# Projections behind the twelfth tile in quarters of the array, with row maxima in single banks beside them

## The chip, the cores and the metric

The kernel runs on one core of one Trainium2 chip. The metric is the device time of one execution, in microseconds. Times of the kernel before come from three runs; durations of single instructions come from one further execution, taken by the hardware profiler. The engines are called PE (TensorE, matrix products), DVE (VectorE), ACT (ScalarE), POOL (GpSimd) and SP (SyncE, which issues most transfers). PSUM has eight banks of 512 float32 for each of 128 partitions; "bank" below is one of these.

## What is computed

Two attention blocks over the same input x (2048 rows, 448 columns, 16 heads of 28), mixed row by row with a gate.

```python
g = sigmoid((x * gate_w).sum(-1))
# A: sliding local attention: 8 keys at distances 0, 2, .. 14
# B: full attention: every row against all 2048 keys
out = g * A(x, A_wqkv, A_wo) + (1 - g) * B(x, B_wqkv, B_wo)
```

Each block projects x with a 448 x 1344 matrix to queries, keys and values, takes a softmax of the scaled scores, and projects the result with a 448 x 448 matrix.

## The kernel before, in words

**Exactness.** PE multiplies in a short format, so every float32 operand is split into a high part (an ACT copy to that format) and a low part (the remainder, a subtraction on DVE or POOL). A projection is a sum of high x high, high x low and low x high.

**Stages.** After ten matmuls on zeros come the projections, then the main loop of 256 steps (scores at L1061, exponential on ACT at L1066, the product with V at L1027, with block A's work on DVE and POOL beside them), then the output projection (L895). An order written out by hand (`manual_schedule`) sets what each engine runs; each engine runs its instructions in the order in which the code writes them.

**Tiles.** The projections are 92 tiles, each 128 rows of PSUM by one bank. First 28 "qk" tiles (queries and keys of block B, transposed, 512 columns; 12 with weight set 0, 12 with set 1, 4 with set 2), then 16 "v" tiles (448 columns) and 48 "a" tiles (block A, 448 columns; the first 16 with two more for the gate). A tile is 11 products (`ORDER`) over the four pieces of the 448 input columns. The last tile is done by `last_tile` inside the main loop.

**Full and halves.** Tiles 0 to 9 (`FULL` = 10) use the whole array, a tile in one bank (`project`). From tile 10 on, `project_halves` splits each product in two of 64 rows, which run in the array's two halves side by side. The halves add into two banks of a pair `PJ`; there are 21 half products for a tile. ACT copies both banks out (L382 for qk, L403 for v and a), POOL adds the two halves (L384, L404, and L407 for the gate). For a qk tile ACT then makes the high part (L387) and POOL the low part (L388), one tile later, and two transfers store them.

**Row maxima.** Pass 1 of block B's softmax needs, for each of 1024 pieces (128 queries by 512 keys, one head), the maximum along the keys: one matmul (`s1_mm`, L153) into a bank and a DVE reduce. 320 of the 1024 are done beside the half products, four for each tile, as 64-row matmuls (`s1_half`): two on each half, in two-bank pairs `PM`, so one DVE reduce (L175) takes two banks. The other 704 run in the main loop (L153, reduces at L159). Every 64 maxima are combined (`max_parts`, L188 and L194 to L196) and turned and stored (`max_turn`, `max_store`).

**Weights.** Six further weight sets are loaded, and split by ACT (L240) and POOL (L241), tile by tile by the tables `loads` and `splits`.

## Time and profile before

| | |
|---|---|
| median of 3 runs | 895.21 us (895.15 to 895.33) |
| span of the profiled execution | 893.6 us |
| PE busy | 889.5 us, 100% |
| DVE busy | 742.3 us, 83% |
| ACT busy | 642.5 us, 72% |
| POOL busy | 642.6 us, 72% |
| first half tile on PE | about 31.4 us after the span's start |
| first main-loop matmul | 248.49 us |

The profiled execution's own time is its span; the times of the runs also hold what lies around it, 1.6 us here. A busy share is an average over stages with different limits, so the rows below are cut by stage. An instruction's duration in the trace runs from its start to its end; matmuls follow each other faster than that, since they are pipelined and run side by side in parts of the array. "Idle before" is an engine's idle time just before a group of instructions, with what ended it.

### The profile page before, as it was taken

The numbers are of one execution on the slowest core, as the hardware profiler recorded it, in microseconds if no ns is written. First come the engines' busy times: TensorE is split into PE (matmuls) and PEld (weight loads), VectorE is DVE, ScalarE is ACT, GpSimd is POOL, SyncE is SP. The second block draws the span as 40 slices with busy tenths as digits, with TensorE's granted clock in tenths as the row PEclk, the third lists the DMA queues.
The fourth block names the chain that finished last, engine by engine and source line by source line (L and its number), as shares of the span: only waits on it lengthen the run. The fifth ranks groups of instructions, "written<-read, shape, count | busy, mean of one in ns | idle before, by whom it ended". The sixth has DMA issues, their size and how long they took to land.

```text
span 893.6 us, 20540 instructions
## 1 busy us (share of the span) xinstructions
PE 889.5 (100%) x8318; PEld 530.0 (59%) x8318; DVE 742.3 (83%) x968; ACT 642.5 (72%) x765; POOL 642.6 (72%) x507
## 2 busy tenths in 40 slices
PE   9999999999999999999999999999999999999998
PEld 7889999999954444444444444444444444434997
DVE  7688999999979999999999999999999999832221
ACT  7456434343378898898988989989889898897220
POOL 1499856464469789998999989999999799701000
PEclk9999999999999999999999999999999999999999
DMA  8886403454372241225224322443121322437681
GB/s 262 267 284 180 157 12 84 135 138 124 100 252 66 90 137 48 65 64 154 74 56 141 89 58 90 126 95 102 46 61 32 92 43 46 107 79 212 179 279 52
DMA packets 114182, 104.51 MB, mean 117 GB/s; under 512 B 75256, under 2 KB 82424, under 8 KB 113304
## 3 DMA queue, kind: packets, MB, share of 16 engines
q1 hardware_dynamic: 113656, 102.42, 40.4%
q8 instruction: 65, 1.06, 0.5%
q10 hardware_dynamic: 432, 0.79, 0.3%
q14 instruction: 29, 0.24, 0.1%
HBM read 62.20 MB, written 40.96 MB: 115 GB/s over the span
## 4 chain that ended last, share of the span: by engine, by line
PE 99%; ACT 0%; issue 0%; DVE 0%; ACTq 0%
PE T L1061 31%; PE av L1027 28%; PE r L331 14%; PE r L326 8%; PE T L895 8%; PE r L153 5%; PE T L153 4%; PE r L226 1%; PE av L478 0%; ACT P L1066 0%; ACT onhi L952 0%; DVE res L1016 0%; ACT L L688 0%; ACTq L952 0%
## 5 line engine op out<-in xcount | busy, mean ns | idle before, releaser
L1066 ACT ACTIVATE P<-T 128x1024 f32<-128x1024 f32 x512 | 496.9, 1024 | 58.3 <-PE T L1061 56.1
L159 DVE TENSOR_REDUCE MX<-T 128x1 f32<-128x512 f32 x470 | 442.2, 953 | 31.3 <-PE T L153 18.8
L1027 PE MATMUL av<-P,V 128*32 128x512 f32 x2048 | 272.7, 605 | 0.0
L1061 PEld LDWEIGHTS T<-QH,KH 30*128 30x128 f32 x1024 | 92.2, 181 | 228.9 <-ACT P L1066 196.5
L153 PE MATMUL T<-KH,QP 30*128 30x512 f32 x704 | 220.9, 458 | 0.1
L1061 PE MATMUL T<-QH,KH 30*128 30x512 f32 x1024 | 211.3, 488 | 0.2 <-ACT P L1066 0.2
L175 DVE TENSOR_REDUCE MX<-r 128x2 f32<-128x1024 f32 x160 | 192.8, 1220 | 20.2 <-PE r L153 16.6
L1061 PE MATMUL T<-QH,KL 30*128 30x512 f32 x1024 | 185.7, 393 | 0.0
L1061 PE MATMUL T<-QL,KH 30*128 30x512 f32 x1024 | 183.0, 389 | 0.0
L662 POOL TENSOR_TENSOR prod<-qt,kt 128x896 f32<-128x896 f32 x64 | 135.4, 2115 | 4.4 <-DMA kt<-a_scr 4.4
L403 ACT ACTIVATE raw<-r 128x896 f32<-128x896 f32 (+1 forms) x62 | 57.1, 921 | 94.5 <-PE r L331 91.8
L153 PE MATMUL r<-KH,QP 64*128 64x512 f32 x320 | 112.9, 391 | 0.0
L723 POOL TENSOR_TENSOR oat<-oat,prod 128x896 f32<-128x896 f32 x48 | 101.4, 2112 | 2.0
L153 PEld LDWEIGHTS T<-KH,QP 30*128 30x128 f32 x704 | 86.0, 181 | 26.4 <-ACT P L1066 15.6
L331 PE MATMUL r<-wh,xh 64*128 64x448 f32 (+1 forms) x504 | 97.9, 363 | 0.0
L718 POOL TENSOR_TENSOR prod<-vt,L 128x896 f32<-128x896 f32 x56 | 95.5, 1706 | 0.3
L404 POOL TENSOR_TENSOR ast<-raw 128x448 f32<-128x448 f32 x47 | 54.3, 1155 | 56.3 <-ACT raw L403 45.8
L1061 PEld LDWEIGHTS T<-QL,KH 30*128 30x128 f32 x1024 | 93.9, 184 | 0.0
L1061 PEld LDWEIGHTS T<-QH,KL 30*128 30x128 f32 x1024 | 92.9, 182 | 0.2
L1027 PEld LDWEIGHTS av<-P,V 128*32 128x32 f32 x2048 | 40.3, 107 | 77.9 <-issue 65.3
L331 PEld LDWEIGHTS r<-wh,xh 64*128 64x128 f32 x504 | 77.5, 185 | 1.5
L331 PE MATMUL r<-wl,xh 64*128 64x448 f32 (+1 forms) x441 | 77.3, 365 | 0.0
(127 smaller groups left out, 1141.3 us busy)
## 6 DMA issues: line engine op xcount, KB each, us to landing
a_scr<-ast SPq DMA_DIRECT2D x24, 448.0 KB
qk_hi<-qkh SPq DMA_DIRECT2D x24, 256.0 KB
qk_lo<-qkh SPq DMA_DIRECT2D x24, 256.0 KB
rbc<-rs SPq DMA_DIRECT2D x64, 64.0 KB
QP<-qk_hi SPq DMA_DIRECT2D x64, 56.0 KB
KL<-qk_lo SPq DMA_DIRECT2D x16, 224.0 KB
QH<-qk_hi SPq DMA_DIRECT2D x64, 56.0 KB
QL<-qk_lo SPq DMA_DIRECT2D x64, 56.0 KB
```

The source lines that it names most:

```text
L153: nc.tensor.matmul(bank, qhis[u][h % 2][r, 128 * qs:128 * qs + 128], KH[u // NB % 3][r, 512 * kc:512 * kc + 512], start=True, stop=True)
L159: i = nc.vector.tensor_reduce(MX[:, n % NMX:n % NMX + k], bank, axis=X, op=ALU.max)
L175: nc.vector.tensor_reduce(m, PM[k], axis=X, op=ALU.max)
L326: nc.tensor.matmul(bank, ws[c][rows, k, t[4]:t[4] + 128], x, start=first, stop=last)
L331: nc.tensor.matmul(bank[:, 0:cols], x, ws[c][rows, k, 0:cols], start=first, stop=last)
L662: nc.gpsimd.tensor_tensor(out=p, in0=qt[c], in1=kvt["k", c % 2][:, HALO - DIL * w:HALO - DIL * w + NJ, :], op=ALU.mult)
L718: nc.gpsimd.tensor_tensor(out=dst.rearrange("p j (h d) -> p j h d", d=DH), in0=kvt["v", c % 2][:, HALO - DIL * w:HALO - DIL * w + NJ, :].r ...
L723: nc.gpsimd.tensor_tensor(out=ows[c % 2][:, :, 0:56] if w == W - 1 else oat[c], in0=oat[c], in1=oat[c, w], op=ALU.add)
L895: writes(bank, nc.tensor.matmul(bank[:, cols], src, wo[c][k][:, cols], start=(first and k == ks[0] and i == 0), stop=(last and k == ks[-1] ...
L1027: nc.tensor.matmul(av[32 * h:32 * h + 32, :], V[:, kt, 4 * g + h, :], tiles_[h], start=(kt == 0), stop=(kt == NJ - 1), skip_group_check=True)
L1061: nc.tensor.matmul(bank[a], (KH[g % 3], KH[g % 3], KL[g % 2])[t][r, ks], (qh, ql, qh)[t][r, :], start=(t == 0), stop=(t == 2))
L1066: e = nc.scalar.activation(p, one if a == "2" else mine, AF.Exp, scale=SCALE).ins
```

## The change

**Quarters.** `FULL` becomes 12. From tile 12 to 90 (79 tiles: 16 qk, 63 v and a) each product is split in quarters of 32 rows; 42 quarter products make a tile. All add into one bank. A tile visits the four quarters of the array one after the other, in an order that a planner (`quarters`) works out when the program is built, and up to six tiles are on their way at a time. Before the first product in the next quarter may write into the bank, the last one of the quarter that the tile leaves must be done: `product` puts a `nop` on POOL that waits for the one, and makes the other wait for that `nop` (`follows`), 237 times.

**Banks.** The PSUM tiles of the stage become eight single banks. A finished tile is copied by ACT straight to its place (`copy_tile`, L452; `qk_tile`, L446 and L447); nothing is added on POOL. The low parts of qk tiles and of weight sets 2 to 6 are made in two halves on POOL (`low_part`, L253), put into the order 32 and 42 products later, the stores 43 products later.

**Maxima.** The 320 maxima become 32-row matmuls, one quarter each (`s1_quarter`, L152), each into a bank of its own with its own reduce of 512 columns (L172).

**Loads.** The tables `loads` and `splits` move by some tiles; weight set 2 lives in the room of `KL[0]`. Two memsets are cut into pieces.

```diff
-        [128, 2, 512], F32, name=f"r{i}") for i in range(4)]
-    PJ, PM = PS[0:2], PS[2:4]
+        [128, 512], F32, name=f"r{i}") for i in range(8)]
...
+    def s1_quarter(h, bank):
+        n = 4 * count[h] + h
+        s1_mm(n, bank)
+        nc.vector.tensor_reduce(MX[:, n % NMX:n % NMX + 1], bank, axis=X, op=ALU.max)
+        count[h] += 1
...
+        def low_part(lo, raw, hi):
+            c = lo.shape[-1] // 2
+            for i, p in enumerate((slice(0, c), slice(c, lo.shape[-1]))):
+                soon(32 + 10 * i, lambda p=p: nc.gpsimd.tensor_tensor(
+                    out=lo[:, p], in0=raw[:, p], in1=hi[:, p].bitcast(F32), op=ALU.subtract))
...
+            rows = slice(0, 128) if q is None else slice(32 * q, 32 * q + 32)
...
+            if q is not None:
+                if n in moved:
+                    follows(i, moved.pop(n))
+                if leaves:
+                    moved[n] = nc.gpsimd.nop()
+                    follows(moved[n], i)
...
+        def quarter_order(n, q):
+            t = tiles[n]
+            low = (t[2] if t[1] == "qk" else t[-1] // 4) < 2
+            return [p for p in ORDER if p != (0, 1, 3) or q // 2 == (0 if low else 1)]
+
+        def quarters(n0, n1, maxima):
+            SLOT, LAT, COPY, FLIGHT = 552, 1030, 1400, 6
...
+                if b is not None and sent[q] < maxima // 4 and sent[q] == min(sent) and sums <= now_ + LAT + 900:
+                    sent[q] += 1
+                    sums = max(sums, now_ + LAT) + COPY + 40
+                    bank[b] = sums + 200
+                    cost = SLOT
+                    yield "max", q, b
...
+                        ready = [f for f in flying if f["in"] is None and f["left"][q] and f["next"] <= now_]
...
+                    if not f["left"][q]:
+                        f.update({"in": None, "next": now_ + (6 if tiles[f["n"]][1] == "qk" else 4) * SLOT})
...
-            raw = pair("raw")
-            nc.scalar.activation(raw, PJ[n % 2], AF.Copy)
-            r = raw[:, 0, :]
-            nc.gpsimd.tensor_tensor(out=r, in0=r, in1=raw[:, 1, :], op=ALU.add)
...
+            raw = ptile("raw")
+            nc.scalar.activation(raw, bank, AF.Copy)
+            nc.scalar.activation(hi, raw, AF.Copy)
+            low_part(lo, raw, hi)
+            soon(43, lambda: qk_store(nb, rows, hi, lo))
+
+        def copy_tile(bank, dst):
+            nc.scalar.activation(dst, bank[:, 0:D].rearrange("p (c e) -> p c e", e=dst.shape[-1]), AF.Copy)
...
-        FULL, S1_START = 10, 10
+        FULL, MAXIMA = 12, 320
...
-        loads = {2: 12, 3: 16, 4: 26, 5: 40, 6: 56}
-        splits = {1: (9, 2), 2: (20, 2), 3: (24, 2), 4: (34, 1), 5: (48, 1), 6: (64, 1)}
+        loads = {2: 10, 3: 13, 4: 22, 5: 38, 6: 54}
+        splits = {1: (9, 2), 2: (15, 2), 3: (18, 1), 4: (33, 1), 5: (48, 1), 6: (64, 1)}
```

**On PE, among the a tiles.** r0 and r1 are the pairs `PJ`, r2 and r3 the pairs `PM`; x2 to x7 are neighbours that alternate between the two halves. Before:

```order
L331 MATMUL r1_132<-wh5_1802,xl2_193 128x448
L153 MATMUL r3_140<-KH0_151,QP11_160 128x512 x2
L331 MATMUL r1_132<-wh5_1802,xl2_193 128x448 x5
L331 MATMUL r0_128<-wh5_1802,xh0_187 128x448 x4
L153 MATMUL r2_136<-KH0_151,QP10_159 128x512 x2
L331 MATMUL r0_128<-wh5_1802,xh0_187 128x448 x4
L331 MATMUL r0_128<-wl5_1803,xh0_187 128x448 x7
L331 MATMUL r0_128<-wh5_1802,xl0_191 128x448
```

And now; r0 to r7 are the eight single banks, and neighbours work in different quarters:

```order
L350 MATMUL r3_140<-wh4_1984,xl2_209 128x450
L350 MATMUL r6_152<-wh4_1984,xh1_204 128x450
L350 MATMUL r2_136<-wh4_1984,xl1_208 128x450
L350 MATMUL r0_128<-wh4_1984,xh3_206 128x450
L152 MATMUL r7_156<-KH0_167,QP00_173 128x512
L350 MATMUL r6_152<-wl4_1985,xh1_204 128x450
L350 MATMUL r1_132<-wh4_1984,xh3_206 128x450
L350 MATMUL r0_128<-wl4_1985,xh3_206 128x450
L350 MATMUL r3_140<-wh4_1984,xl2_209 128x450
L152 MATMUL r5_148<-KH0_167,QP00_173 128x512
```

A maximum stands alone among the products of four tiles, where two stood together between those of one or two.

**On DVE, in the middle of the stage.** Before, the reduces alternate between the two pairs:

```order
L175 TENSOR_REDUCE MX_154<-r2_136 128x2
L175 TENSOR_REDUCE MX_154<-r3_140 128x2
L175 TENSOR_REDUCE MX_154<-r2_136 128x2
L175 TENSOR_REDUCE MX_154<-r3_140 128x2
L175 TENSOR_REDUCE MX_154<-r2_136 128x2
```

And now, by single banks that the planner found free:

```order
L172 TENSOR_REDUCE MX_170<-r7_156 128x1
L172 TENSOR_REDUCE MX_170<-r0_128 128x1
L172 TENSOR_REDUCE MX_170<-r7_156 128x1
L172 TENSOR_REDUCE MX_170<-r0_128 128x1
L172 TENSOR_REDUCE MX_170<-r7_156 128x1
L172 TENSOR_REDUCE MX_170<-r4_144 128x1
L172 TENSOR_REDUCE MX_170<-r0_128 128x1
```

Mostly two banks alternate here; in the whole stage 228 of the 320 maxima go to the bank of the maximum two before.

**On ACT, at the first qk tiles of the new stage.** Before, one raw copy of two banks and one high part for each tile, with the splits of weight set 2 between:

```order
L240 ACTIVATE wh2_817<-raw_525 128x128 x2
L382 ACTIVATE raw_852<-r0_128 128x1024
L387 ACTIVATE qkh_809<-raw_810 128x512
L240 ACTIVATE wh2_817<-raw_525 128x128
L240 ACTIVATE wh2_817<-wt_526 128x128
L382 ACTIVATE raw_890<-r1_132 128x1024
```

And now, for six tiles that end within 60 matmuls of each other:

```order
L446 ACTIVATE raw_787<-r1_132 128x512
L447 ACTIVATE qkh_786<-raw_787 128x512
L446 ACTIVATE raw_787<-r4_144 128x512
L447 ACTIVATE qkh_814<-raw_787 128x512
L446 ACTIVATE raw_845<-r5_148 128x512
L447 ACTIVATE qkh_844<-raw_845 128x512
L321 ACTIVATE KL0_169<-raw_467 128x128 x2
L446 ACTIVATE raw_845<-r2_136 128x512
L447 ACTIVATE qkh_852<-raw_845 128x512
```

The raw copy is of one bank, the high part stands right behind it, and the splits (now into `KL0`) stand among six tiles in a row. From the first main-loop matmul on, every engine's rows are the same as before.

## Rows read from the trace of the kernel before

**Rows 1.** Windows by stage; busy us and count per engine, PEclk, DMA share, GB/s.

```profile
11.10:31.40 20.30, 20.30 (x89) 16.33 (x87) 13.76 (x21) 13.37 (x25) 1.04 (x2) 1.00 0.88 281
31.40:83.60 52.20, 52.20 (x451) 43.99 (x452) 43.25 (x38) 29.75 (x45) 46.02 (x41) 1.00 0.81 252
83.60:248.40 164.80, 164.80 (x1575) 160.84 (x1571) 151.28 (x135) 66.39 (x86) 98.41 (x105) 1.00 0.39 109
248.40:893.60 645.20, 641.84 (x6178) 301.45 (x6177) 526.36 (x757) 526.78 (x597) 492.92 (x354) 1.00 0.37 101
```

**Rows 2.** Groups of 31.4 to 248.4: count, busy us, mean ns, idle before.

```profile
L175 DVE TENSOR_REDUCE MX<-r 128x2 f32<-128x1024 f32 x160 | 192.8, 1220 | 20.2 <-PE r L153 16.6 <-PE r L326 0.8 <-PE r L331 0.2
...
L403 ACT ACTIVATE raw<-r 128x896 f32<-128x896 f32 x46 | 42.3, 920 | 69.5 <-PE r L331 68.2 <-POOL nmt L196 1.3
...
L388 POOL TENSOR_TENSOR qkh<-raw,qkh 128x512 fp32r<-128x512 f32 x18 | 23.7, 1317 | 0.0
...
L387 ACT ACTIVATE qkh<-raw 128x512 fp32r<-128x512 f32 x18 | 11.2, 623 | 4.9 <-POOL raw L384 4.9
...
L240 ACT ACTIVATE wh<-raw 128x448 fp32r<-128x448 f32 x9 | 5.0, 569 | 0.0
...
L188 DVE TENSOR_REDUCE m<-MX 128x16 f32<-128x64 f32 x4 | 1.1, 270 | 0.1
```

**Rows 3.** Timeline of PE in the main loop: start us, us.

```profile
371.69 0.40 PE L1061 MATMUL T<-QL,KH 30*128 30x512 f32 x2
371.78 0.50 PE L1061 MATMUL T<-QH,KH 30*128 30x512 f32 x2
371.92 0.40 PE L1061 MATMUL T<-QH,KL 30*128 30x512 f32 x2
372.12 0.40 PE L1061 MATMUL T<-QL,KH 30*128 30x512 f32 x2
372.14 0.46 PE L153 MATMUL T<-KH,QP 30*128 30x512 f32 x2
```

**Rows 4.** Groups of the whole trace: DVE's one-bank reduces, ACT's one-bank copies.

```profile
L159 DVE TENSOR_REDUCE MX<-T 128x1 f32<-128x512 f32 x236 | 161.9, 686 | 24.0 <-PE T L153 18.5 <-PE T L1061 3.0
```

```profile
L377 ACT ACTIVATE qkh<-r 128x512 fp32r<-128x512 f32 x10 | 5.8, 594 | 5.8 <-PE r L326 3.8 <-DMA qk_lo<-qkh 1.9
```

**Rows 5.** Timeline of DVE early in the half stage.

```profile
40.13 2.39 DVE L175 TENSOR_REDUCE MX<-r 128x2 f32<-128x1024 f32 x2 [0.40 <-PE r L153]
```

**Rows 6.** Timeline of DVE: three subtractions; then two reduces, 512 and 1024 columns.

```profile
16.23 1.90 DVE L241 TENSOR_TENSOR xl<-V,xh 128x512 fp32r<-128x512 f32 x3
...
403.76 1.81 DVE L159 TENSOR_REDUCE MX<-T 128x1 f32<-128x512 f32 x2
```

**Rows 7.** Timeline of all engines where ACT frees a bank, then PE fills one.

```profile
253.48 1.94 ACT L1066 ACTIVATE P<-T 128x1024 f32<-128x1024 f32 x2 [0.41 <-PE T L1061]
...
255.48 0.50 PE L153 MATMUL T<-KH,QP 30*128 30x512 f32 x2
...
255.50 0.48 PE L1061 MATMUL T<-QH,KL 30*128 30x512 f32 x2
...
256.02 1.23 DVE L159 TENSOR_REDUCE MX<-T 128x2 f32<-128x1024 f32 x1 [0.20 <-PE T L1061]
```

**Rows 8.** Timeline of ACT: two weight splits of 128 columns.

```profile
62.47 0.50 ACT L240 ACTIVATE wh<-raw 128x128 fp32r<-128x128 f32 x2
```

**Rows 9.** Line L384 in 77 to 86: its waits in POOL's sequencer, its operations.

```profile
L384 POOLq EVENT_SEMAPHORE  x4: 43/43/43, 77.9 to 80.9; - x4
L384 POOL TENSOR_TENSOR raw<-raw x3: 1344/1350/1351, 78.5 to 85.8; 128x512 f32<-128x512 f32 x3
```

**Rows 10.** Timeline of all engines at the main loop's start.

```profile
248.49 0.18 PEld L1061 LDWEIGHTS T<-QH,KH 30*128 30x128 f32 x2 [0.31 <-issue]
...
248.68 0.55 ACT L399 ACTIVATE raw<-r 128x448 f32<-128x448 f32 x1 [1.16 <-PE r L331]
...
249.50 0.21 PEld L153 LDWEIGHTS T<-KH,QP 30*128 30x128 f32 x2 [0.48 <-ACT raw L399]
```

More of the change, by code (lines that the diff above doesn't have):

```diff
@@ L143, in load_qhi, with s1_mm @@
             dma_r(qhis[u][h % 2][32 * h:32 * h + DH, :], qk_hi[r:r + DH, 512 * b:512 * b + 512])
-    def s1_mm(n, bank, half=False):
+    def s1_mm(n, bank):
         u, i = divmod(n, 64)
@@ L316, in gated_mix_kernel, with product @@
                   (1, 0, 1), (1, 0, 2)]
-        def product(n, p, half, first, last):
+        def product(n, p, q, bank, first, last, leaves=False):
             t = tiles[n]
             ws = wsets[t[0]]
-            rows = slice(0, 128) if half is None else slice(64 * half, 64 * half + 64)
-            bank = PS[n % 4][:, 0, :] if half is None else PJ[n % 2][:, half, :]
+            rows = slice(0, 128) if q is None else slice(32 * q, 32 * q + 32)
             a, c, k = p
@@ L325, in product @@
                 x = (xh[t[2]], xl[t[2]])[a][rows, k, :]
-                nc.tensor.matmul(bank, ws[c][rows, k, t[4]:t[4] + 128], x, start=first, stop=last)
+                i = nc.tensor.matmul(bank, ws[c][rows, k, t[4]:t[4] + 128], x, start=first, stop=last)
             else:
@@ L330, in product, with follows @@
                 x = (xh[j // 4], xl[j // 4])[a][rows, k, 128 * (j % 4):128 * (j % 4) + 128]
-                nc.tensor.matmul(bank[:, 0:cols], x, ws[c][rows, k, 0:cols], start=first, stop=last)
+                i = nc.tensor.matmul(bank[:, 0:cols], x, ws[c][rows, k, 0:cols], start=first, stop=last)
+            if q is not None:
[4 more added lines that the diff above has]
+                    follows(moved[n], i)
+        moved = {}
+        def follows(i, j):
+            tc.add_manual_dep(i.ins, j.ins.name, mybir.DependencyInfo(
+                mybir.DependencyClass.Sync, mybir.DependencyReason.DATA), reason="other rows, same bank")
         def project(n):
@@ L339, in project @@
                 for i, p in enumerate(order):
-                    product(n, p, None, i == 0, i == len(order) - 1)
-        todo = [[], []]
-        def project_halves(n, s1):
-            if n % 2 == 0:
-                for m in (n, n + 1)[:len(tiles) - 1 - n]:
-                    low = (tiles[m][2] if tiles[m][1] == "qk" else tiles[m][-1] // 4) < 2
-                    for half in range(2):
-                        l = [p for p in ORDER if p != (0, 1, 3) or half == (0 if low else 1)]
-                        l = [(m, product, (m, p, half, i == 0, i == len(l) - 1)) for i, p in enumerate(l)]
-                        if s1[m - n]:
-                            l[8:8] = [(m, s1_half, (1, half))]
-                            l[2:2] = [(m, s1_half, (0, half))]
-                        todo[half] += l
-            while any(l and l[0][0] == n for l in todo):
-                for l in todo:
-                    if l:
-                        _, f, x = l.pop(0)
-                        f(*x)
+                    product(n, p, None, PS[n % 4], i == 0, i == len(order) - 1)
@@ L420, in gated_mix_kernel @@
+            if s is not None:
+                j -= j % 2
+                nc.sync.dma_start(a_own[i][:, :, j:j + 2, :].rearrange("c p j e -> p c j e"), stage.pop(k))
         QK = [[[(0, 128)], [(448, 576)], [(576, 704)]],
@@ L520, in gated_mix_kernel @@
                     nc.scalar.activation(t, t0, AF.Copy)
-            while fini and fini[0][0] <= n:
-                fini.pop(0)[1]()
             if n == 2:
@@ L531, in gated_mix_kernel @@
             if n == 40:
-                init_kl(KL[0])
+                for i in range(4):
+                    soon(20 * i, lambda i=i: init_kl(KL[0][:, 512 * i:512 * i + 512]))
             if n == 16:
@@ L565, in gated_mix_kernel @@
                 load_q(0)
+        gate = []
+        for n in range(FULL):
+            before(n)
+            project(n)
+            if n == 0:
+                split_x(1, (3,))
+            for m in {0: (), 1: (0, 1)}.get(n, (n,)):
+                finish(m, PS[m % 4], n)
+            behind(n)
+        n = FULL
+        before(n)
+        for kind, *x in quarters(FULL, len(tiles) - 1, MAXIMA):
+            if kind == "max":
+                s1_quarter(x[0], PS[x[1]])
+            elif kind == "product":
+                product(*x[:3], PS[x[3]], *x[4:])
+                sent[0] += 1
+                run_queue()
+            else:
+                finish(x[0], PS[x[1]], n)
+                behind(n)
+                n += 1
+                before(n)
+        assert not queue
     hooks = {}
```

150 lines of the change are left out of this document (83 added, 67 removed).

## The prediction

> **What bounds the kernel now.** I read the program in stages first. Between 31.4 us, where the projections go over to halves of the array, and 248.4, where the main loop starts, TensorE is busy without a gap at a full granted clock [rows 1]. The main loop behind it is as before in every row of every engine, so only the time at which it starts can move, and the 645.2 us from there to the end stay. In the half stage DVE is the second: 192.8 us of two-bank reduces, with 20.2 us of idle time in which it waits for TensorE's maxima [rows 2]. ACT, too, waits for TensorE: 68.2 us before 46 of its copies [rows 2]. So TensorE sets the pace, and DVE has a tenth of the stage to spare.
>
> **The cost of a tile before.** Two half products run side by side. The 164.8 us from 83.6 to 248.4 hold the last 63 tiles of the stage [rows 1], 2.616 us each. The 18 qk tiles take 52.2/18 = 2.90 us each, 12.5 slots of 0.232 (10.5 of products, two of 64-row maxima); with such slots for its maxima a v or a tile has (2.616 - 0.463)/10.5 = 0.205 for a slot of two products.
>
> **Two more full tiles.** Ten full tiles end at 31.4 and the last eight of them took 20.30 us [rows 1], 2.54 each. Two more put the start of the new stage at 31.4 + 5.1 = 36.5.
>
> **TensorE in quarters.** The new stage has 16 qk tiles and 63 others, 42 quarter products each, and 320 maxima. The trace has products of 30 rows and 512 columns in the main loop: eight of them start from 371.69 on, the ninth at 372.14 [rows 3], so four cost 0.225. I take 0.2275 for four of 512 columns, between that and the 0.232 of a half slot. For 448 columns the bounds are 0.201 (the same less 64 columns at 2.4 GHz, the granted clock being 1.00) and 0.2055, the half slot. Sum: (672 + 320)/4 x 0.2275 = 56.4, plus 2646/4 x (0.201 to 0.2055) = 133.0 to 135.9: 189.4 to 192.3 us. By TensorE alone the main loop would start at about 227 to 230, some 20 us earlier.
>
> **DVE takes over as the bound.** The maxima become 320 reduces of one bank instead of 160 of two. One of 512 columns takes 0.686 us, one of 1024 takes 1.220 [rows 2, 4]; alone, a pair costs 1.37 instead of 1.22. How close can they follow each other? Two-bank reduces with no wait between take 2.39 the pair [rows 5], an overlap of 0.05; a one-bank and a two-bank reduce took 1.81, against 0.686 + 1.220, an overlap of 0.10 [rows 2, 4, 6]; three 512-column subtractions took 1.90, (1.90 - 0.69)/2 = 0.605 from start to start [rows 6]. I take 0.605 for a reduce whose successor is ready. But in the new order 228 of the 320 maxima use the bank of the maximum two before, so TensorE may write only when that reduce is over. The cycle on one bank is the reduce, 0.69, the way to TensorE, 0.05 (exponential ends 255.42, matmul starts 255.48), a matmul of 0.50, and 0.04 to DVE (255.98 to 256.02) [rows 7], 1.28 for two maxima, 0.64 each. Sum: 228 x 0.64 + 92 x 0.605 = 201.6 us; with a successor always ready 320 x 0.605 = 193.6; with every maximum alone on DVE (0.69 + 0.05) 236.8. I take 201.6, since the order alternates two banks for seven in ten. Other DVE work of the stage I put at 2.5 us, of which four sums of maxima at L188 are 1.1 [rows 2].
>
> On this the Trainium skill speaks against the change: "VectorE: DVE Perf Modes", § The DRAIN you can't avoid, says that after each operation the next does not start until the pipe is empty, and "TensorEngine Tiling (Array Packing)", § PSUM Bottleneck, that tiling speeds up TensorE and not the emptying of PSUM, which should span several tiles. The 1.90 for three speaks for an overlap; by the first rule the sum would be the fourth rival's, and by the second 320 x 0.686 = 219.5 takes the place of 160 x 1.220 = 195.2, which is near it.
>
> **ACT.** For a v or a tile a copy of 896 columns (0.920 [rows 2]) becomes one of 448 (about 0.55 [rows 10]), straight to its place; that only frees ACT. For a qk tile it has a raw copy of 512 columns, 0.594 [rows 4], and the high part, 0.623 [rows 2]. But four to six tiles in flight end close together: the first six qk tiles end at matmuls 231 to 291 of the stage, 3.3 us at 0.0555 each, while ACT needs 6 x 1.22 + 4 x 0.30 (four weight splits, 0.50 for two with overlap [rows 8]) = 8.5. TensorE asks for the last of their six banks at matmul 338, 5.9 us behind the first end; the last raw copy is done at 8.5 - 0.6 = 7.9: a wait of 2.0. The second burst (494 to 588) has four splits of 0.57 [rows 2] but lasts longer; I put 2 at it too. A TensorE wait starves DVE, except for one or two maxima that are ready; I take 2.5 of the 4, and keep 0 to 4.6.
>
> **POOL.** Its additions of halves go; what stays are low parts in halves, which TensorE waits for only as weights. It gets 237 no-operations: each product that leaves a quarter signals POOL's sequencer, that signals back, and the tile's first product in its next quarter waits for it. Queued in front are POOL's own waits; behind stands TensorE's whole in-order stream. The way is the product (up to 0.50 [rows 7]), 0.04, a semaphore step of 0.043 [rows 9], and 0.05 back: 0.63 us. The order leaves mostly 17 or more matmuls, 0.94 us. In the trace POOL's sequencer takes waits from 77.9 on for operations that run up to 85.8 [rows 9], so it runs ahead of the queue, and a queued operation need not hold the signal. I cost it at nothing, with an upper end: if it does hold, eleven low parts (6.2 us by halves of 1.317 [rows 2]) stand before the nineteenth signal and nine (4.7) before the twenty-first, some 5 us in all beyond the room; if the way were 0.1 longer than the room each time, 237 x 0.1 = 24.
>
> **The end of the stage.** The last maximum is matmul 3613 of 3638, so TensorE ends as the last reduce does, within 0.1. Then the main loop's first matmul waits for the last copy: 0.40 [rows 3] + 0.04 + 0.55 + 0.05 = 1.0, where before it had 0.31 and, a microsecond later, 0.48 behind the same copy [rows 10]; the 0.48 goes. SP's loads move by a few tiles and land behind nothing that TensorE waits for: 0.
>
> **Sum.** 36.5 + 0.5 (first maximum) + 201.6 + 2.5 + 2.5 + 0.1 + 1.0 - 0.5 = 244.2, against 248.5 [rows 10]: -4.3 us. The profiled execution spans 893.6, the median of the runs is 895.21, so 1.6 lie outside; the comparison is a difference, and 895.2 - 4.3 = 890.9.
>
> **Rivals.**
> 1. DVE is always fed, since a max has eight banks to choose from and TensorE, 10 us faster than DVE, runs ahead: 193.6 and no lost stalls, -4.3 - 8.0 - 2.5 = -14.8, 880.4; with the stalls 882.9. For it: the spare TensorE time. Against: the two-bank alternation.
> 2. The other side: the reduces come at a longer pitch than the cycle, because a maximum sits between products that wait, in an in-order stream, with one bank of slack. It decides at (201.6 + 4.3)/320 = 0.643 us per maximum; at 0.66 it is +5.3, 900.5; at 0.74 it is +31. For it: DVE waited 0.40 us for TensorE again and again before [rows 5]. Against: TensorE then was the bound.
> 3. The signal through POOL is late: +5 by the held queue, 896; more if the way is longer than the room.
> 4. No overlap of reduces at all: 320 x 0.69 = 220.8, 19.2 above the sum's term, 910. Against: 1.90 and 1.81 [rows 6]. It is the rule of "VectorE: DVE Perf Modes" named above.
> 5. The quarters don't run four deep, that is, the change doesn't do what it says. TensorE then bounds from a mean slot of 205.9/909.5 = 0.226 us on, where I reckon 0.208 to 0.211; at 0.25 it is +21.5, 917. Against: [rows 3], where weight loads and products of four quarters overlap.
>
> **How the numbers follow.** What can be told from no change is 0.2%, 1.8 us, so "same" is 893.4 to 897.0. The forecast has 0.42, rival 1 0.17, rival 2 0.20 (half of it in "same", half slower), rival 3 0.12 (0.07 same, 0.05 slower), rival 4 0.06, rival 5 0.03. Faster 0.59, same 0.17, slower 0.24. The range reaches from rival 1 with its stalls to rival 2 at 0.66: 882 to 900.5; outside are rivals 4, 5, the far ends of 2 and 3 and the lowest of 1, 0.2 together. Where faster cases alone are taken, 882 to 893.4.
>
> **What would show it.** Right: in the new stage DVE is busy over 95% with few and short waits, TensorE shows small waits for DVE and two clusters of waits for ACT's raw copies about 13 and 28 us into it; the main loop starts at about 244. A mean start-to-start of reduces near 0.63 is the term that matters most. Wrong: DVE's idle time ended by TensorE in many small pieces (rival 2), TensorE waits that end with POOL (rival 3), a reduce pitch of 0.69 with no idle (rival 4), or TensorE without waits and a later main loop (rival 5). If the main loop's own length changed, the premise would fall.

## The result: 0.4% slower, and the profile after

The changed kernel takes 899.16 us (median of 5 runs, 898.45 to 900.58) where the one before takes 895.24; the ratio is 1.0043, with a 95% interval of 1.003 to 1.0055. The forecast was 890.9. The profiled execution took 899.5 us and spans 897.7.

The stages of the profiled execution, to be read against [rows 1]: the full tiles from 11.10 on; the stretch to the last product of a qk tile ("the qk part"); from there to the main loop ("the v and a part"); the main loop. Columns as there: PE, PEld, DVE, ACT, POOL busy with counts, PEclk, DMA share, GB/s.

```profile
11.10:36.96 25.86, 25.86 (x114) 20.73 (x112) 15.51 (x25) 15.56 (x28) 3.88 (x4) 1.00 0.89 285
36.96:94.70 57.74, 57.23 (x855) 47.66 (x855) 53.64 (x85) 20.44 (x40) 26.35 (x45) 1.00 0.70 210
94.70:252.78 158.08, 156.76 (x2791) 145.44 (x2785) 152.14 (x248) 42.70 (x102) 22.74 (x40) 1.00 0.41 111
252.78:897.70 644.92, 641.65 (x6177) 301.59 (x6177) 526.27 (x756) 526.00 (x596) 491.45 (x352) 1.00 0.37 102
```

The main loop takes 644.9 us, 645.2 before, so all of the loss lies ahead of it: it starts at 252.78 instead of 248.5. The cut at 94.70 does not divide the tiles cleanly, since up to six run side by side: in the planner's order 98 products of v tiles, 2.3 tiles' worth, and 84 maxima stand ahead of the last qk product. What is left, 2548 products or 60.7 tiles, takes 158.08 us, 2.61 us for a v or a tile, where the halves took 2.616: they break even. With 2.3 tiles at that price taken off, the 16 qk tiles cost (57.74 - 6.1)/16 = 3.23 us each, where the halves needed 2.90. That is where the change loses, some 5 us; the two more full tiles, cheaper than halves, give 0.2 back.

The groups of DVE in the quarter stage, against the L175 row of [rows 2], and those of its first reduces that run without a gap:

```profile
L172 DVE TENSOR_REDUCE MX<-r 128x1 f32<-128x512 f32 x320 | 204.3, 687 | 6.8 <-PE r L152 4.8 <-PE r L345 0.9
L185 DVE TENSOR_REDUCE m<-MX 128x16 f32<-128x64 f32 x4 | 1.0, 258 | 0.0
```

```profile
37.70 0.69 DVE L442 TENSOR_TENSOR qkh<-r,qkh 128x512 fp32r<-128x512 f32 x1 [1.85 <-ACT qkh L441]
38.30 13.66 DVE L172 TENSOR_REDUCE MX<-r 128x1 f32<-128x512 f32 x21
```

DVE is busy nearly all the time, but slowly: 21 reduces in 13.66 us are (13.66 - 0.69)/20 = 0.649 from start to start. Over all 320 the mean is 0.6625. With the next bank ready a step is 0.597 or 0.598 (43 of the 319; seven are shorter, down to 0.544). A reduce is 0.687 long, longer than the mean step, so a step that grows from 0.60 to 0.66 leaves DVE no idle time: its busy share does not show the loss.

What a maximum does to TensorE is seen on one of them. This is the timeline of PE, its weight loads (PEld) and DVE around 100.3 us:

```profile
99.61 0.69 DVE L172 TENSOR_REDUCE MX<-r 128x1 f32<-128x512 f32 x1
...
100.05 0.19 PEld L350 LDWEIGHTS r<-wl,xh 32*128 32x128 f32 x1
100.19 0.36 PE L350 MATMUL r<-wh,xh 32*128 32x448 f32 x1
100.24 0.69 DVE L172 TENSOR_REDUCE MX<-r 128x1 f32<-128x512 f32 x1
100.26 0.36 PE L350 MATMUL r<-wl,xh 32*128 32x448 f32 x1
100.35 0.18 PEld L152 LDWEIGHTS r<-KH,QP 30*128 30x128 f32 x1
100.36 0.50 PE L152 MATMUL r<-KH,QP 30*128 30x512 f32 x1
100.36 0.19 PEld L350 LDWEIGHTS r<-wh,xh 32*128 32x128 f32 x2
100.36 0.47 PE L350 MATMUL r<-wh,xh 32*128 32x448 f32 x2
100.36 0.18 PEld L350 LDWEIGHTS r<-wl,xh 32*128 32x128 f32 x1
100.89 0.69 DVE L172 TENSOR_REDUCE MX<-r 128x1 f32<-128x512 f32 x1
```

The reduce that began at 99.61 ends at 100.30 and frees the bank; the maximum's weights are loaded 0.05 later, its matmul is 0.50 long, and the reduce of it starts at 100.89 (the one at 100.24 reads the other bank). Between 100.05 and 100.35 no weights are loaded for any quarter: the products of the other three stand behind the maximum in TensorE's one queue. They all begin together at 100.36, and the products beside the maximum take 0.47 instead of 0.36. Counted over the stage's trace, 216 of the 228 maxima that use the bank of two before load their weights 0.052 to 0.054 us after that bank's reduce. The profile hardly calls this a wait, since older products are still running: the waits that it lists for TensorE in the stage are small.

```profile
PEld r L152 <- DVE MX L172: 3.6, 15, 0.4
...
PEld r L152 <- ACT raw L446: 1.2, 3, 0.6
...
PEld r L350 <- POOLq L355: 1.0, 1, 1.0
...
PEld r L350 <- POOL wl L253: 0.7, 1, 0.7
```

### The profile page after: what moved, and what is told of

Its sections match the earlier page's. It is cut to its first block, busy times and chain, and to the rows that moved or that the text cites. A ratio compares the mean times of both kernels' runs of the same rounds, so it can differ in the third digit from the quotient of the medians.

```text
span 897.7 us, 24157 instructions
## 1 busy us (share of the span) xinstructions
PE 891.6 (99%) x9957; PEld 522.4 (58%) x9957; DVE 754.9 (84%) x1129; ACT 610.9 (68%) x779; POOL 548.6 (61%) x448
## 3 DMA queue, kind: packets, MB, share of 16 engines
q8 instruction: 78, 1.28, 0.6%
## 4 chain that ended last, share of the span: by engine, by line
PE 96%; ACT 1%; DMA 1%; issue 1%; POOL 1%; DVE 0%; ACTq 0%; POOLq 0%
PE T L1130 30%; PE av L1096 28%; PE r L350 15%; PE T L964 8%; PE r L345 6%; PE T L152 4%; PE r L152 4%; DMA V<-in_xT 1%; POOL qkh L253 0%; PE av L527 0%; POOL wl L253 0%; DVE MX L172 0%; ACT P L1135 0%; DMA qk_hi<-qkh 0%; ACT raw L446 0%
## 5 line engine op out<-in xcount | busy, mean ns | idle before, releaser
L1135 ACT ACTIVATE P<-T 128x1024 f32<-128x1024 f32 x512 | 497.0, 1024 | 59.1 <-PE T L1130 56.9
L152 PE MATMUL T<-KH,QP 30*128 30x512 f32 x704 | 220.8, 458 | 0.0
L172 DVE TENSOR_REDUCE MX<-r 128x1 f32<-128x512 f32 x320 | 204.3, 687 | 6.8 <-PE r L152 4.8
L350 PE MATMUL r<-wh,xh 32*128 32x448 f32 (+1 forms) x1008 | 158.8, 370 | 0.7 <-POOLq L355 0.7
L350 PE MATMUL r<-wl,xh 32*128 32x448 f32 (+1 forms) x882 | 151.7, 367 | 0.3 <-POOL wl L253 0.3
L350 PE MATMUL r<-wh,xl 32*128 32x448 f32 (+1 forms) x756 | 142.6, 365 | 0.0
L152 PE MATMUL r<-KH,QP 30*128 30x512 f32 x320 | 133.2, 433 | 0.2
L350 PEld LDWEIGHTS r<-wh,xh 32*128 32x128 f32 x1008 | 124.1, 183 | 3.6 <-POOLq L355 1.0
L350 PEld LDWEIGHTS r<-wl,xh 32*128 32x128 f32 x882 | 116.2, 184 | 1.2 <-POOL wl L253 0.7
L350 PEld LDWEIGHTS r<-wh,xl 32*128 32x128 f32 x756 | 105.0, 184 | 0.4
L152 PEld LDWEIGHTS T<-KH,QP 30*128 30x128 f32 x704 | 86.0, 181 | 25.7 <-ACT P L1135 15.9
```

The source lines that it names most:

```text
L152: nc.tensor.matmul(bank, qhis[u][h % 2][r, 128 * qs:128 * qs + 128], KH[u // NB % 3][r, 512 * kc:512 * kc + 512], start=True, stop=True)
L172: nc.vector.tensor_reduce(MX[:, n % NMX:n % NMX + 1], bank, axis=X, op=ALU.max)
L350: i = nc.tensor.matmul(bank[:, 0:cols], x, ws[c][rows, k, 0:cols], start=first, stop=last)
L1135: e = nc.scalar.activation(p, one if a == "2" else mine, AF.Exp, scale=SCALE).ins
```

## The experiments

Each edit is one against the changed kernel unless another is named. Times of before are those of the runs beside it, 895.2 to 895.5. A table of the profiled executions stands first, read from their timelines: us from the span's start, each the start of the instruction named; the last column is the median of the runs. Four kernels (e1_half_reduce, e2_no_maxima, e10_half_reentry, e12_light_qk_half) have a single run each; they and e11_light_qk leave part of the result out, to find a cause.

| run | first product in quarters | last qk product | last reduce | main loop | time |
|---|---|---|---|---|---|
| changed kernel | 36.96 | 94.68 | 249.65 | 252.78 | 899.2 |
| e1_half_reduce | 37.31 | 92.07 | 240.27 | 243.96 | 892.2 |
| e2_no_maxima | 36.36 | 90.08 | none | 229.66 | 877.8 |
| e3_flight5 | 36.99 | 98.83 | 238.77 | 254.32 | 902.5 |
| e4_reentry | 36.66 | 92.65 | 245.78 | 247.66 | 896.6 |
| e5_full10 | 31.61 | 91.62 | 244.98 | 253.38 | 904.8 |
| e6_low_later | 36.88 | 94.35 | 248.83 | 251.96 | 899.8 |
| e7_spread | 36.47 | 94.16 | 248.74 | 251.85 | 899.5 |
| x_combo | 31.55 | 91.84 | 240.55 | 249.34 | 896.0 |
| e10_half_reentry | 36.67 | 90.57 | 241.46 | 243.08 | 890.5 |
| e11_light_qk | 36.72 | 92.62 | 247.90 | 250.93 | 899.6 |
| e12_light_qk_half | 36.91 | 89.67 | 237.67 | 241.32 | 889.5 |
| h_62 | 84.11 | in halves | 242.26 | 243.86 | 891.6 |
| h_52 | 83.94 | in halves | 241.52 | 252.12 | 902.2 |
| h_63 | 84.15 | in halves | 244.47 | 247.43 | 895.2 |

### Is it DVE's cycle on a bank, or TensorE?

**e1_half_reduce.**

```diff
-        nc.vector.tensor_reduce(MX[:, n % NMX:n % NMX + 1], bank, axis=X, op=ALU.max)
+        nc.vector.tensor_reduce(MX[:, n % NMX:n % NMX + 1], bank[:, 0:256], axis=X, op=ALU.max)
```

> The changed kernel, but each of the 320 reduces of the quarter stage reads 256 of its bank's 512 columns (half of the keys are left out of those maxima). The order of every engine stays. Theory A, the cycle on a bank (reduce, way to TensorE, matmul, way to DVE) bounds the stage: a reduce falls from 0.69 to about 0.4 us, the cycle of two banks from 1.27 to about 0.98, 0.49 per maximum, and TensorE takes over: its 192 us of products and maxima and about 8 of other waits put the main loop's first matmul near 237 instead of 252.8, and the time near 884. Theory B, TensorE in quarters is slower of itself (products that do not overlap four deep, signals through POOL): the time stays within 3 us of the changed kernel's 899.

The single run: 892.2 us. Its DVE group:

```profile
L172 DVE TENSOR_REDUCE MX<-r 128x1 f32<-128x256 f32 x320 | 133.2, 424 | 67.3 <-PE r L152 40.5 <-PE r L350 15.1 <-PE r L345 6.2
```

DVE now waits 67.3 us, 61.8 of them for TensorE, and the stage is still 206.7 us long (37.31 to 243.96). So neither theory held alone. Cheaper reduces give 9 us back: that is DVE's share. With them TensorE needs 206.7 where 191 was reckoned. The two parts of this run show how that is spread:

```profile
37.31:92.07 54.76, 54.42 (x854) 49.22 (x855) 35.22 (x85) 20.30 (x40) 26.09 (x44) 1.00 0.71 213
92.07:243.96 151.89, 151.16 (x2791) 148.00 (x2785) 100.08 (x247) 42.43 (x103) 22.89 (x41) 1.00 0.43 117
```

By the prediction's own slots (0.2275 for four of 512 columns, 0.203 for four of 448) the qk part, with 672 products of qk tiles, 84 maxima and the 98 products of v tiles that run in it, should take 756/4 x 0.2275 + 98/4 x 0.203 = 48.0. It takes 54.8. The v and a part should take 2548/4 x 0.203 + 236/4 x 0.2275 = 142.7, and takes 150.9 to its last product. TensorE's sum was short in both parts, by 6.8 and by 8.2 us, in proportion more for the qk tiles (14% for 6%). The price of a slot has little of this: matched to the planner's order, two products of one tile in one quarter follow each other at 0.233 (512 columns) and 0.205 (448 columns) in the median. Most of the 15 us is time in which a quarter has no product to start.

**e2_no_maxima.** The matmuls and reduces of the stage's maxima are left out, `s1_quarter` only counts.

> The changed kernel without the 320 maxima of the quarter stage (neither their matmuls nor their reduces; those values are zeros). Products, copies, low parts and signals stay in their order. Theory A: TensorE needs 3318 products x 0.0515 = 171 us and about 6 of waits for ACT and POOL; main loop near 214, the time near 861. Theory B: products in quarters cost more than reckoned, 0.0564 each as the v and a part now shows, and the qk part its 9 us of waits: main loop near 233, the time near 879.

The single run: 877.8 us, near the second number. Without a single maximum the v and a part takes 138.6 us to its last product where the same slots give 129.3, and the qk part 53.7 where they give 43.2: 9.3 and 10.5 us too long, with DVE out of the matter. Two gaps in the qk part are plain. This is the longer, on the timeline of weight loads:

```profile
54.21 0.18 PEld L347 LDWEIGHTS r<-xh,wh 32*128 32x128 f32 x1
56.13 0.28 PEld L347 LDWEIGHTS r<-xh,wh 32*128 32x128 f32 x3 [1.74 <-POOLq L357]
```

```profile
36.36:90.08 53.72, 51.51 (x771) 47.69 (x774) 1.22 (x4) 19.98 (x40) 25.84 (x44) 0.94 0.74 225
```

The signal through POOL came 1.74 us late, behind a burst of ten halves of low parts that POOL worked on from 50.71 to 56.02, which is the third rival's mechanism. And the granted clock of the part is 0.94 here: after that gap, and after one of 0.67 us at 75.91, it stood at 1.2 instead of 2.4 GHz for 3.4 us. In the changed kernel, where TensorE runs behind DVE, the wait at the same place (60.33) is only 0.19 us and the clock stays at 1.00.

### More banks, or sooner re-entry

**e3_flight5.**

```diff
-            SLOT, LAT, COPY, FLIGHT = 552, 1030, 1400, 6
+            SLOT, LAT, COPY, FLIGHT = 552, 1030, 1400, 5
```

> One number of the planner: at most five tiles on their way instead of six, so one more bank is there for maxima (68 instead of 228 of the 320 maxima go to the bank of the maximum two before, 184 to that of three before). Theory A: the mean start to start of reduces falls from 0.662 towards 0.61, up to 16 us less; five tiles for four quarters give some of it back in waits for the signal between quarters: 887 to 895. Theory B (TensorE bound): fewer tiles only mean more waits, 900 or more.

902.45 us, ratio to before 1.0074 (1.0057 to 1.0091). The third bank does for DVE what was expected: the mean step of reduces falls from 0.6625 to 0.628. DVE's timeline at the end:

```profile
235.67 3.78 DVE L172 TENSOR_REDUCE MX<-r 128x1 f32<-128x512 f32 x6
239.49 0.27 DVE L185 TENSOR_REDUCE m<-MX 128x16 f32<-128x64 f32 x1
240.68 0.21 DVE L202 STREAM_TRANSPOSE nms<-nmt 128x32 f32<-128x32 f32 x1 [0.93 <-POOL nmt L193]
254.94 0.69 DVE L158 TENSOR_REDUCE MX<-T 128x1 f32<-128x512 f32 x1 [14.05 <-PE T L152]
```

The maxima are done at 239.5, ten us sooner than in the changed kernel, and then DVE waits 14 us: TensorE has products left. That five tiles leave more quarters empty would explain it; it was not counted. A bank given to DVE is taken from TensorE.

**e4_reentry.**

```diff
-                        f.update({"in": None, "next": now_ + (6 if tiles[f["n"]][1] == "qk" else 4) * SLOT})
+                        f.update({"in": None, "next": now_ + (3 if tiles[f["n"]][1] == "qk" else 2) * SLOT})
```

> One rule of the planner: a tile may enter its next quarter 3 slots (qk) or 2 slots (v, a) behind its last product instead of 6 or 4, so tiles end sooner and hold their banks for less time; 152 instead of 228 maxima go to the bank of two before. Theory A with a quick signal (0.63 us): 2 slots are 0.41 to 0.46 us, so many signals come late by 0.2, but banks are freer; 893 to 901. If POOL's signal is a heavy cost (the rival of the prediction), the shorter room shows it: over 905.

896.57 us, ratio 1.0012 (1.0003 to 1.0021): 2.6 us better than the changed kernel, within the first range. The main loop starts 5.1 us sooner, at 247.66, with a mean step of 0.651; its own length is then 647.2 instead of 644.9, with TensorE at half its clock for 3.4 us from 250.06 on, 2.4 us behind the wait for the last copies:

```profile
247.66:265.00 17.34, 16.97 (x144) 8.92 (x146) 11.30 (x13) 12.58 (x15) 7.22 (x12) 0.90 0.81 265
```

The signal through POOL does not make 237 costly steps: with room for two slots it would have shown. But it is late in five places, 4.7 us of waits of weight loads, the longest 1.97 at 60.98, where the changed kernel has 1.4 in all.

**e5_full10.** `FULL, MAXIMA = 10, 320`.

> One number of the changed kernel undone: 10 full tiles instead of 12, so the quarter stage and its maxima begin two tiles (5.1 us) sooner. Theory A, DVE's maxima (one bank back, two banks in turn) set the length of the stage: about 211 us of maxima follow from about 33 instead of 38.3, the main loop starts 3 to 5 us sooner, 894 to 896. Theory B, TensorE sets it: two tiles in quarters cost what two full ones did, 5.1 to 5.3 us, and the time stays at 898 to 900.

904.79 us, ratio 1.0106 (1.0089 to 1.0123). Slower still, and both theories miss. DVE did start and end 5 us sooner (last reduce 244.98), as the first says, but the main loop starts later, at 253.38: TensorE has 8 us of products left behind the last maximum. Two more qk tiles in quarters cost 6.0 us: the stage starts 36.96 - 31.61 = 5.35 sooner without the two full ones, and ends 0.6 later. The main loop itself is 648.2 us long instead of 644.9, with the clock at half for 3.4 us from 256.24 on. This alone does not tell a dear qk tile from a worse order.

### POOL's part

**e6_low_later.** In the changed kernel this is what stood at 125 us, on the timelines of DVE, ACT, POOL and PE:

```profile
124.25 0.37 PE L350 MATMUL r<-wl,xh 32*128 32x448 f32 x1
125.33 0.47 PE L350 MATMUL r<-wh,xh 32*128 32x448 f32 x2 [0.69 <-POOLq L355]
```

```profile
124.61 0.26 DVE L185 TENSOR_REDUCE m<-MX 128x16 f32<-128x64 f32 x1
124.78 0.68 DVE L172 TENSOR_REDUCE MX<-r 128x1 f32<-128x512 f32 x1
124.89 0.22 ACT L191 ACTIVATE nmt<-m 128x16 fp32r<-128x16 f32 x1 [0.60 <-DVE m L185]
125.02 0.20 ACT L192 ACTIVATE nmv<-m 128x16 f32<-128x16 f32 x1
125.12 0.52 ACT L452 ACTIVATE V<-r 128x448 f32<-128x448 f32 x1
125.29 0.22 POOL L193 TENSOR_TENSOR nmt<-nmv,nmt 128x16 fp32r<-128x16 f32 x1 [9.97 <-ACT nmv L192]
```

POOL's small subtraction at L193 waits for ACT, which waits for DVE's L185, which stands behind all reduces before it. A no-operation behind L193 cannot pass, and TensorE waits at the product that needs it.

```diff
-                parts.append((n + 3, u, max_parts(u)))
+                parts.append((n + 3, u, max_parts(u, lambda f: soon(32, f))))
```

> In the quarter stage the low part of each 64 combined maxima goes into POOL's order 16 products later, so POOL does not sit at a wait for ACT (and through it for DVE's queue) with the signals between quarters behind it. Theory: that wait is what ends TensorE's 1.17 us gap at 125 us, and smaller ones at the other three places; 1 to 2 us less, 897 to 898.2. Rival: the gap has another cause, or the time goes to DVE's reduces, which were the later ones anyway: within 0.5 us of 899.

The expectation says 16 products later; the kernel that ran has 32. The waits of TensorE for POOL's sequencer fall from 2.1 us in the trace to 0.2, and the main loop starts 0.8 us sooner. The runs do not show it: 899.80 us, ratio 1.0048 (1.0033 to 1.0063). The cause of the gap is shown; its price is below 1 us, probably since DVE's reduces were late anyway.

**e7_spread.** As e6_low_later, but 16 products later, and the low parts at least 8 products apart (4 for the smallest):

```diff
-                soon(32 + 10 * i, lambda p=p: nc.gpsimd.tensor_tensor(
+                turn[0] = max(turn[0] + (8 if c > 100 else 4), sent[0] + 32)
+                soon(turn[0] - sent[0], lambda p=p: nc.gpsimd.tensor_tensor(
```

> As e6_low_later, and the low parts of qk tiles and weights stand at least 8 products apart in POOL's order instead of in bursts of up to eleven. Theory: the signals that were held behind a burst (0.4 us at 60 in the changed kernel, up to 2 us where TensorE ran ahead) come in time, 1 to 2 us less than e6_low_later, 895.5 to 897.5. Rival: in the qk part the copies of ACT and DVE's cycle are as late as POOL, so nothing is won over e6_low_later; a weight's low part that is now later could cost up to 1 us more.

899.47 us, ratio 1.0048 (1.0033 to 1.0063); main loop at 251.85, as in e6_low_later. The rival was right: nothing is won over it.

**x_combo.** e4_reentry, e5_full10, e6_low_later and e7_spread together.

> Four edits together: 10 full tiles, re-entry behind 3 and 2 slots, the low part of the maxima later, the low parts spread. If they add up (e5_full10 -4, e4_reentry -2.6, the other two -2 to -4): 889 to 892, below the kernel before. If TensorE's waits for DVE's cycle take back what the others give: 894 to 897.

896.03 us, ratio 1.0004 (0.9993 to 1.0015): the second range. With the shorter re-entry ten full tiles cost no more than twelve.

### What holds the qk part

**e10_half_reentry.** The edits of e1_half_reduce and e4_reentry.

> e1_half_reduce (reduces of 256 of 512 columns, half of the keys left out) with the shorter re-entry of e4_reentry. It tells how much of TensorE's 206.7 us between the stage's first product and the main loop in e1_half_reduce, against 191 reckoned, is quarters standing empty because the order keeps a tile out for 4 to 6 slots. If that is most of it: 196 to 200 us, main loop near 234 to 237, time 882 to 885. If it is ACT's and POOL's work and bursts: within 3 us of e1_half_reduce's 892.

The single run: 890.5 us, stage 206.4 us, as long as in e1_half_reduce. So a shorter distance between quarters does not bring 206.7 towards 191. Whether the distance is free is not shown: with it shortened TensorE's weight loads wait 4.1 us for POOL's signal and 2.1 for copies of v tiles, where e1_half_reduce has 0.9 and none, and these could hide a gain. That e4_reentry won through banks that come free sooner fits its 152 maxima on the bank of two before, instead of 228, but was not tested alone.

**e11_light_qk.**

```diff
-            raw = ptile("raw")
-            nc.scalar.activation(raw, bank, AF.Copy)
-            nc.scalar.activation(hi, raw, AF.Copy)
-            low_part(lo, raw, hi)
+            nc.scalar.activation(hi, bank, AF.Copy)
+            soon(32, lambda: nc.gpsimd.memset(lo.bitcast(F32), 0.0))
```

> The changed kernel with little work behind its 16 qk tiles in quarters: ACT makes the high part straight from the bank (one copy instead of two) and POOL writes zeros in one piece instead of two subtractions (the low parts of these queries and keys are left out). If the bursts of copies and low parts cost the qk part its time: 57.7 us becomes 52 to 54, main loop near 248, the time near 895. If DVE's cycle on a bank holds that part: within 1.5 us of the changed kernel's 899.

899.60 us, ratio 1.0047 (1.003 to 1.0064); qk part 55.9 instead of 57.7, main loop at 250.93. The bursts behind the qk tiles cost 1.8 us there. The median of the runs shows none of it, but three of its four runs have a granted clock of 0.996 or 0.997; the one at 0.999 took 897.63, where the changed kernel's four at 0.999 and 1.0 took 898.45 to 899.5.

**e12_light_qk_half.** The edits of e11_light_qk and e1_half_reduce.

> e11_light_qk with the reduces of e1_half_reduce (256 of 512 columns): neither DVE nor ACT nor POOL should hold TensorE then. If waits for these three are all that TensorE loses: qk part 44 to 47 us (43 reckoned), stage 193 to 196 instead of 206.7, the time near 880. If the order itself leaves quarters empty in the qk part: 50 us or more there, the time near 886 to 889.

The single run: 889.5 us, half a microsecond above the second case. Its qk part:

```profile
36.91:89.67 52.76, 52.76 (x854) 49.97 (x855) 35.20 (x86) 11.87 (x26) 14.61 (x32) 1.00 0.77 234
```

TensorE has no gap at all here, ACT and POOL have about half their work, the reduces are short, and the 854 matmuls still take 52.8 us instead of 48.0 (the 43 of the expectation leaves out the 98 products of v tiles, as do its signs for the two cases). The v and a part takes 150.7 for 142.7, as in e1_half_reduce. So of the 15 us that TensorE's sum is short there, the work of ACT and POOL behind the qk tiles makes about 2; 13 are left, 5 in the qk part and 8 in the v and a part. With all three other engines light, the order of one queue for four quarters is the likely maker of them. Which rule of the planner makes them was not found.

### A version with only the v and a tiles in quarters

**h_62.** Tiles 10 to 27 as before, in halves with two-bank reduces; the 63 v and a tiles in quarters, re-entry behind 2 slots, the low part of the maxima 16 products later, the sets' tables as before up to set 3.

```diff
-        FULL, MAXIMA = 12, 320
+        FULL, HALF, MAXIMA = 10, 28, 320
...
+        for n in range(FULL, HALF):
+            before(n)
+            project_halves(n, (True, True))
+            qk_tile(n, None, n, *tiles[n][2:4])
+            behind(n)
+        tctx[0].close()
+        tctx[0] = ExitStack()
+        PS[:] = [tctx[0].enter_context(tc.tile_pool(name=f"pq{i}", bufs=1, space=bass.MemoryType.PSUM)).tile(
+            [128, 512], F32, name=f"q{i}") for i in range(8)]
+        done = s1c[0]
+        count[:] = [done // 4] * 4
...
+        for kind, *x in quarters(HALF, len(tiles) - 1, MAXIMA - done):
```

> Half of the change undone: tiles 0 to 9 full and the 18 qk tiles 10 to 27 in halves with two-bank reduces, as before; only the 63 v and a tiles in quarters, with 248 maxima, re-entry behind 2 slots, six tiles on their way. If the qk part is where quarters lose (57.7 us for 16 tiles against 52.2 for 18) and the v and a part goes as in e4_reentry (153 us against 164.8): main loop near 239 instead of 248.5, 886 to 889. If the loss lies in DVE's cycle on a bank wherever quarters run: v and a part 158 to 162, 891 to 894.

891.56 us (891.39 to 891.98), ratio to before 0.9956 (0.9941 to 0.9971): faster than both kernels, 3.9 us below the one and 7.6 below the other. Its stages:

```profile
31.40:84.11 52.71, 52.71 (x452) 44.17 (x451) 43.78 (x38) 29.76 (x45) 46.54 (x41) 1.00 0.80 245
84.11:243.86 159.75, 159.25 (x2893) 148.48 (x2894) 156.38 (x259) 42.54 (x102) 27.14 (x43) 1.00 0.43 115
243.86:889.80 645.94, 642.50 (x6182) 301.92 (x6180) 526.07 (x756) 526.59 (x597) 491.57 (x352) 1.00 0.36 101
```

The halves take 52.7 us for 52.2 before; the v and a part takes 159.75 us against 164.80 in [rows 1], 2.54 us a tile. In the changed kernel these tiles broke even at 2.61, so it is not enough to leave the qk tiles in halves: the shorter re-entry comes in too (h_63). Its reduces come 0.638 apart and DVE idles 2.5 us before them: DVE's cycle holds the part, as the second case said, and the time lies just in that case's range.

**h_52** and **h_63.** One number each of h_62: five tiles on their way; re-entry behind 3 slots.

> As h_62 with five tiles on their way instead of six, so that a third bank is there for most maxima (154 instead of 87 go to the bank of three before). If the bank cycle counts for more than empty quarters: 1 to 3 us less than h_62. If TensorE in quarters needs six tiles: 2 to 4 us more.

> h_62 with re-entry behind 3 slots instead of 2: the signal has more room, but more quarters stand empty and 3 maxima in 10 more use the bank of two before. Between 0.5 us less and 2 us more than h_62's 891.6.

902.24 us, ratio 1.0069 (1.0052 to 1.0086), and 895.18, ratio 1.0007 (0.9998 to 1.0017). h_52 repeats e3_flight5: reduces end at 242.2, the main loop waits for TensorE's products until 252.12, and from 250.20 on, still among the last of these, the clock is at half for 10.2 us. In h_63 the last reduce starts 2.2 us later than in h_62 and the main loop 3.6; its v and a part takes 163.28, 2.59 us a tile. The order that the planner finds is touchy: one slot of re-entry is worth 3.6 us, about as much as the whole change lost.

## Why the prediction was wrong, step by step

**The premise held.** The main loop is 644.9 us long, 645.2 before.

**Two more full tiles: nearly.** The quarter stage starts at 36.96, not 36.5. The first reduce is at 38.30, not 37.0: DVE still had the low part of the last full tile [the L442 row above]. That step, costed at 0.5, is 1.3.

**DVE's term: right in kind, short in size.** The alternation of two banks is what the order made of it, and the cycle that I built from [rows 7] is what happens: reduce 0.69, way 0.053, matmul, way 0.04. The sum of 1.28 for two left out that the quarter which the maximum goes to may still be at work: its matmul starts 0.07 us after its weights on the average, up to 0.23, and is 0.44 long. Two maxima take 1.305 in the v and a part, 1.375 in the qk part. From the first reduce's start to the last one's end DVE took 249.65 + 0.69 - 38.30 = 212.0, where 201.6 + 2.5 + 2.5 = 206.6 stood. That is 5.4 of the 8.6 us by which the main loop missed its time (252.78 for 244.2); the first reduce's start has 1.3 of the rest and the end 1.9. A step of 0.6625 is beyond the point, 0.643, that the second rival named, and 0.66 was its example, at 900.5. That rival came true, in its number and in its in-order stream; it had a chance of 0.20 and half of that in "same". The signs that I named did not tell it apart: DVE was busy 95% of the stage with 6.8 us of idle time before its reduces, as I wrote for "right"; only the step itself, 0.6625 for 0.63, did.

**TensorE's term: the step that failed.** 189.4 to 192.3 us were reckoned, and TensorE taken to be some 10 us ahead of DVE. With cheap reduces it needs 206.7 (e1_half_reduce): it had no lead. To the last product these are 205.66 us for 909.5 slots of four, 0.226 each, which is just the slot from which on, by the prediction's fifth rival (chance 0.03), TensorE bounds. About 7 of the 15 us too many lie in the qk part, 8 in the v and a part. Taking the price of [rows 3] from a place where all four quarters always have work, I left out the time in which the order leaves a quarter without any. And I took the longer of two chains as if the other could not touch it. DVE's maxima alone were reckoned at 201.6; from the first reduce to the last one's end the maxima that TensorE delivers to cheap reduces take 240.69 - 38.66 = 202.0; together they take 212.0, since a maximum that waits for its bank stops all four quarters (the timeline above), and a TensorE that is late brings the next maximum late. What in the order leaves the quarters empty stays open.

**ACT's and POOL's bursts: about right, 1.8 us (e11_light_qk) for 2.5.** With cheap reduces they cost 2.0 (52.8 in e12_light_qk_half for 54.8), so DVE's lateness hides little of them. TensorE's waits for raw copies came in two clusters, as said, but at 21 to 23 and 41 to 42 us into the stage instead of 13 and 28, 1.3 us in all.

**The signal through POOL: nearly free, as said.** In the trace the no-operation starts about 0.05 us (median) after the product that it waits for ends, and more than 0.3 us after it 14 times of 237. My text named POOL's waits in front of it but priced only its queued work; the gap at 125 us is such a wait.

**The end: 2.4 us, not 1.1 less 0.5.** Behind the last maximum (matmul at 248.84) the products thin out, since the last tiles must still go through their quarters one after the other: from 249.95 to 250.77 two products start each 0.2 us, where four did before. The wait for the last copy is the 1.0 that was reckoned.

```profile
250.15 0.36 PE L350 MATMUL r<-wh,xh 32*128 32x448 f32 x1
250.16 0.36 PE L350 MATMUL r<-wl,xh 32*128 32x448 f32 x1
250.35 0.36 PE L350 MATMUL r<-wh,xh 32*128 32x448 f32 x1
250.36 0.36 PE L350 MATMUL r<-wh,xl 32*128 32x448 f32 x1
...
252.78 0.50 PE L1130 MATMUL T<-QH,KH 30*128 30x512 f32 x2 [0.63 <-ACT ast L452]
```

**The fourth rival.** With the next bank ready, reduces start 0.598 us apart and are 0.687 long, so they do overlap a little and that rival fell. By the rule that the Trainium skill's "VectorE: DVE Perf Modes", § The DRAIN you can't avoid, begins with, each would start 0.69 after the one before; this trace does not agree. The section goes on that an operation which is not held starts earlier; with that the trace agrees. The reduces take 204.3 us in all where 192.8 stood, while for TensorE, with cheap reduces (e1_half_reduce), a v or a tile takes 151.89/60.7 = 2.50 us instead of 2.616. That tiling speeds up the products and not the emptying of PSUM is said by the Trainium skill's "TensorEngine Tiling (Array Packing)", § PSUM Bottleneck; here the trace agrees.

## What to carry to other kernels

An engine with one queue that feeds several parts of itself loses all of them at each wait. Two chains of about equal length that pass through it take longer than either (here 201.6, as reckoned, and 202.0, with cheap reduces, made 212.0), and a price taken from a place where every part has work is a lower bound. Two buffers in turn bind a fast producer to the whole cycle of the consumer; look for the load that starts right at the consumer's end, even where the profile lists hardly a wait, and at the step from start to start, since the consumer's busy share hides it. Before a rebuild is judged as a whole, cut its result by the kinds of work in it, and by counted instructions: where tiles of two kinds run side by side, a cut in time gives one kind work of the other. Here qk tiles lost 5 us and v and a tiles broke even; of the versions that compute everything, the best is the one that rebuilds only these and lets them re-enter sooner.

## What the runs showed of the hardware that was not expected

**The clock and short waits.** TensorE's granted clock fell to half (1.2 of 2.4 GHz) for 3.4 us, 0.05 to 2.4 us behind the end of gaps of 0.63 to 2.06 us, in the middle of a program that is at 1.00 before and behind: twice in the qk part of e2_no_maxima (0.94 over the part), at 97.18 in x_combo, and soon after the main loop's start in e1_half_reduce, e2_no_maxima, e3_flight5, e4_reentry (0.90 over 17 us), e5_full10, e11_light_qk and e12_light_qk_half; and for 10.2 us in h_52, in the thin end of its products, without a gap. The length of the gap does not tell which one does it: the 0.63 us before the main loop was followed by it in e1_half_reduce and not in the profiled execution of the changed kernel, e6_low_later or e7_spread, and e4_reentry has one of 1.54 us at 59.45 and e10_half_reentry one of 1.59 at 93.47 without it. It also spreads the runs: those of e4_reentry take 895.2 to 895.5 at a mean granted clock of 0.999 or 1.0 and 898.0 at 0.996, those of e6_low_later 898.6 at 1.0 and 900.7 at 0.996. So of two medians that lie 1 or 2 us apart the clocks must be looked at first.

**Reduces by size.** One of 256 columns takes 0.424 us, of 512 0.687, of 1024 1.220: 0.16 us for each and 0.26 for 256 columns.

**Weights behind a wait.** From the end of a reduce to the load of the weights that waited for it there are 0.052 to 0.054 us, 216 times of 228 in the changed kernel.
